# A decayed linear attention with a highway layer behind it: k and q turned in 64-row tiles, q loaded eight tokens to a row, a cap on transfers in flight, and a new order of work

## The chip, the cores and the metric

The kernel runs on one core of a Trainium2 chip. That core has a matrix engine (PE, also TensorE), three engines that work on whole tiles element by element (DVE or VectorE, ACT or ScalarE, POOL or GpSimd), a sequencer that only issues transfers (SP or SyncE), and 16 DMA engines that move data between the chip's main memory and the on-chip memory SBUF. PE reads its operands from SBUF and writes to PSUM, the accumulators, which are divided into banks. Here DVE and ACT read PSUM, and POOL works on SBUF alone.

The metric is the device time of one execution in microseconds (us). Over 13 runs the kernel before takes 109.42 us in the median, 108.25 to 110.27.

## The reference

The inputs are q, k, v of shape 4 batches x 8 heads x 768 tokens x 64, a decay `lam` per head (0.97 to 0.99), two 512 x 512 weights and a bias. Attention is causal and linear, in blocks of 64 tokens with a running state, and the highway layer follows on the 3072 x 512 result.

```python
for b in range(nb):                       # blocks of 64 tokens
    intra = einsum('bhic,bhjc->bhij', qb, kb) * Dmask       # Dmask: lam**(i-j) for i >= j, else 0
    intra = einsum('bhij,bhjd->bhid', intra, vb)
    inter = einsum('bhid,bhde->bhie', qb * lam**(pos+1), kv_state)
    out[:, :, sl] = intra + inter
    kv_state = lam**64 * kv_state + einsum('bhsd,bhse->bhde', kb * lam**(63-pos), vb)
x = out.transpose(0, 2, 1, 3).reshape(3072, 512)
H = maximum(x @ w_h, 0)
T = 1 / (1 + exp(-(x @ w_t + b_t)))
result = T * H + (1 - T) * x
```

## The kernel before

**Stages.** The tokens are cut into 12 stages of 256 tokens, three to a batch, numbered n = 0 to 11. The decay is folded into the operands: q is multiplied by lam to the power of the token's place in its batch and v by lam to the power of minus that place, so the mask has only ones and zeros (`tri`) and the state is a plain running sum, `kv`, which stays in one PSUM bank. A stage has two half-stages b of 128 tokens, and heads are treated in pairs: pair hp is heads 2hp and 2hp+1, and e says which one of the two.

**The order.** Nothing is scheduled by a program. The string `PLAN` is a list of steps, and each engine runs its own steps in the order in which they stand there. A step is `Name.arguments=banks` or `Name.arguments@engine`:

- `Lk`, `Lq`, `Lv`: load half of a stage (256 KB) of k, q or v, all issued by SP in the order of the list; `W`: load half of a weight (512 KB); `ST`: store 256 finished rows (512 KB), also on SP. Five buffers hold raw k, q and v each, so a load can wait for a buffer, and every load behind it on SP then waits as well.
- `CK`, `CQ`, `CV`: cast k to bf16; scale and cast q and v (mostly on POOL). A second argument of 2 means the whole stage. `WC` casts weights.
- `TK`, `TQ`: turn (transpose) k and q on PE by a multiplication with the identity `id128`. One whole-stage step is 8 instructions, each of 128 tokens x 128 features (two heads), which fill all of PE's 128 rows. `EK`, `EQ` copy each PSUM bank of results to SBUF (`kT`, `qT`).
- `SS`: the scores of the head e of all pairs, interleaved with the state update of half-stage 1-e. These are 64 x 64 tiles of PE, so that several can run side by side. `M` multiplies scores by the mask on DVE; `KE` copies the state to SBUF (`ss`).
- `I`: q times state, for each half-stage a group of 4 instructions of 128 columns; `A`: masked scores times v, added to the same bank; `D`: copies the attention output to `xT` in bf16 and puts the tokens back into their order.
- `F.n.u.w`: one block of the highway layer (w=0 for w_h, w=1 for w_t), 8 instructions of 256 columns; `H` (max and subtraction, DVE), `G` (sigmoid, ACT), `X` (product, DVE) follow.
- `R`: turns `xT` + gated part back to token rows, in 64-row tiles: 32 instructions of 64 columns whose two row halves write to two banks; `E` copies to SBUF. The last half-stage goes through `turn`, `evac_o` and `store` instead.
- `Z.n`: n multiplications of no use, which keep PE busy before data is there; `B`, `BC`: the bias as a column; `PT`: loads ACT's sigmoid table.

**What the loads look like.** k, q and v have one partition per two tokens (`J = 2`), so each row that DMA moves is 2 x 64 x 4 = 512 bytes. On SP a load waits, beside its buffer, for the transfer eight places before it, since eight semaphores are used in turn.

**Layouts that matter below.** `qT` is [128 features of a pair, pair, j, 128], so the 128 columns that a score reads are two runs of 64 elements. In `take` (the step `D`) the output is written with a step of two elements, because j is innermost in the token order.

Of the kernel before, what the change touches and what calls it, by code (L numbers as in the profile page):

```python
# [17 lines left out]
Lk.0.0 Lv.0.1 Lv.0.0 Lq.0.0 Lk.0.1 Lq.0.1 Lv.1.1 CK.0.0@POOL Lq.1.0 Z.12=0 TK.0.0=0 Lq.1.1 CV.0.0@DVE Lk.1.0  # L18
CQ.0.0@POOL EK.0.0@DVE Lv.1.0 CV.0.1@DVE CK.0.1@ACT Lk.1.1 Z.11=1 TQ.0.0=1 B=2 EQ.0.0@ACT CQ.0.1@POOL W.0.1 W.0.0
Z.6=0 TQ.0.1=3 TK.0.1=4 EQ.0.1@DVE U.0.0 EK.0.1@ACT W.1.1 S.0.0=56 KE.0.0@DVE S.0.1=01 CQ.1.2@POOL W.1.0 M.0.0.1 Z.1=3  # L20
U.0.1 I.0=34 M.0.1.1 KE.0.1@ACT Lk.2.1 M.0.0.0 A.0.1 M.0.1.0 TQ.1.2=0 Lq.2.1 CV.1.2@DVE CK.1.2@ACT EQ.1.2@ACT Lq.2.0
Z.8=1 TK.1.2=1 A.0.0 EK.1.2@DVE Lk.2.0 D.0.0@DVE Z.3=5 SS.1.1=56 WC.0.0.1@ACT WC.0.0.0@POOL M.1.1.0 KE.1.0@ACT
WC.0.1.0@POOL D.0.1@ACT Lv.2.1 WC.0.1.1@DVE Z.4=0 SS.1.0=01 M.1.1.1 I.1=35 KE.1.1@ACT Lv.2.0 F.0.0.0=4 WC.1.1.0@DVE PT
M.1.0.1 Lk.3.1 F.0.1.0=6 M.1.0.0 WC.1.0.0@POOL WC.1.0.1@ACT Lk.3.0 WC.1.1.1@DVE A.1.1 A.1.0 BC F.0.0.1=1 H.0.1 Lq.3.1
D.1.1@ACT H.0.0 D.1.0@ACT F.0.1.1=0 Lq.3.0 CQ.2.2@POOL F.1.0.0=2 Lv.3.0 G.0.1@ACT CK.2.2@DVE F.1.0.1=6 Lv.3.1
G.0.0@ACT X.0.1@DVE TQ.2.2=5 Lq.4.0 X.0.0@DVE TK.2.2=4 EQ.2.2@ACT CV.2.2@POOL F.1.1.0=3 Lq.4.1 EK.2.2@DVE G.1.0@ACT
H.1.0 SS.2.0=01 Lk.4.1 H.1.1 CK.3.2@POOL SS.2.1=54 Lk.4.0 M.2.0.1 F.1.1.1=2 KE.2.0@ACT M.2.1.0 Lv.4.0 TK.3.2=3 M.2.1.1
CQ.3.2@POOL G.1.1@ACT I.2=15 M.2.0.0 Lv.4.1 A.2.1 X.1.0@DVE A.2.0 Lk.5.0 R.0=40 D.2.0@ACT D.2.1@DVE CV.3.2@POOL
TQ.3.2=6 E.0.0@ACT Lk.5.1 F.2.1.1=1 E.0.1@ACT EQ.3.2@DVE Lq.5.1 EK.3.2@ACT X.1.1@DVE F.2.1.0=5 CQ.4.2@POOL Lq.5.0
R.1=40 H.2.1 SS.3.1=62 Lv.5.0 F.2.0.0=3 CK.4.2@POOL KE.3.0@ACT M.3.1.1 Lv.5.1 E.1.1@ACT M.3.1.0 SS.3.0=52 E.1.0@ACT  # L30
H.2.0 Lq.6.0 TQ.4.2=0 KE.3.1@ACT CV.4.2@POOL M.3.0.1 TK.4.2=6 G.2.1@ACT Lq.6.1 F.2.0.1=4 M.3.0.0 EQ.4.2@ACT EK.4.2@DVE
Lv.6.0 I.3=32 A.3.0 CK.5.2@POOL A.3.1 Lk.6.1 SS.4.1=56 D.3.0@ACT D.3.1@DVE TK.5.2=0 KE.4.0@ACT M.4.1.1 Lk.6.0
F.3.0.0=2 G.2.0@ACT CQ.5.2@POOL EK.5.2@DVE Lv.6.1 SS.4.0=36 H.3.0 F.3.0.1=0 Lq.8.0 M.4.0.0 CV.5.2@POOL M.4.0.1
TQ.5.2=2 Lk.9.0 G.3.0@ACT F.3.1.0=3 X.2.1@DVE Lq.7.0 EQ.5.2@ACT X.2.0@DVE F.3.1.1=6 CQ.6.2@POOL M.4.1.0 Lq.7.1
KE.4.1@ACT I.4=14 H.3.1 G.3.1@ACT R.2=25 Lk.8.1 X.3.0@DVE A.4.0 E.2.1@ACT X.3.1@DVE A.4.1 Lk.7.1 SS.5.0=30 E.2.0@ACT
D.4.0@DVE CK.6.2@POOL SS.5.1=56 D.4.1@ACT Lk.7.0 TQ.6.2=2 M.5.0.0 KE.5.0@ACT CV.6.2@POOL TK.6.2=1 M.5.1.1 Lv.7.0
EQ.6.2@ACT F.4.1.0=4 M.5.0.1 Lv.7.1 EK.6.2@ACT F.4.0.0=3 H.4.1 Lk.8.0 M.5.1.0 I.5=62 SS.6.1=01 H.4.0 Lq.8.1 A.5.0
KE.6.0@ACT M.6.1.0 CQ.7.2@POOL R.3=45 Lv.9.1 A.5.1 M.6.1.1 SS.6.0=30 D.5.0@ACT Lv.8.0 F.4.0.1=1 M.6.0.0 D.5.1@ACT
M.6.0.1 Lk.9.1 TQ.7.2=6 G.4.0@ACT CK.7.2@POOL F.5.0.0=3 Lq.10.1 EQ.7.2@ACT F.4.1.1=2 H.5.0 Lk.10.1 E.3.1@ACT X.4.0@DVE
TK.7.2=0 CV.7.2@POOL G.4.1@ACT I.6=63 ST.0 KE.6.1@DVE F.5.0.1=5 X.4.1@DVE Lv.8.1 F.5.1.0=1 G.5.0@ACT CK.8.2@POOL  # L40
EK.7.2@DVE Lq.9.0 A.6.0 E.3.0@ACT H.5.1 A.6.1 SS.7.1=20 Lq.9.1 D.6.0@ACT D.6.1@DVE TK.8.2=4 M.7.1.1 F.6.1.0=1 Lv.9.0
# [24 lines left out]
def kernel(  # L66
# [13 lines left out]
    C = 128  # L80
# [4 lines left out]
    J = 2  # L85
    N = B * NST
# [12 lines left out]
    def copy(eng, dst, src):  # L99
        if eng == "ACT":  # L100
            A.activation(dst, src, AF.Copy)  # L101
        else:
            ENG[eng].tensor_copy(dst, src)  # L103


    lam_bc = singles.tile([128, H], F32)
    A.dma_start(out=lam_bc, in_=lam.partition_broadcast(128))
    bt_r = singles.tile([KC, 128], F32)
    A.dma_start(out=bt_r, in_=moe_b_t.rearrange("(j p) -> j p", p=128))
    id128 = singles.tile([128, 128], BF16)  # L110
    make_identity(nc, id128)
    blank = singles.tile([128, 512], BF16)
# [306 lines left out]
```

## Time and profile before

| | us or share |
|---|---|
| median of 13 runs | 109.42 |
| the profiled execution, its own time | 109.43 |
| its span, first to last instruction | 107.4 |
| PE busy | 100.0 (93%) |
| DVE busy | 82.3 (77%) |
| ACT busy | 71.8 (67%) |
| POOL busy | 55.7 (52%) |
| moved by DMA | 27.59 MB, of which 20.98 MB read |
| packets under 2 KB | 38712 of 42701 |
| granted PE clock, mean | 0.994 |

The busy time of PE includes the `Z` steps (13.0 us) and modelled ends of matmuls, so it is not the share at which PE does useful work. What a step costs in a row of others is better read from the chain of waits, which gives the time from one step's start to the next one's. DMA busy is the mean over the 16 engines; the shares of the stretches can exceed one since packets on an engine overlap. About 2.0 us of the profiled execution lie outside its span.

### The profile page before, as it was taken

What the parts mean: (1) busy time and instruction counts of PE and PEld (TensorE: products, weight loads), DVE (VectorE), ACT (ScalarE), POOL (GpSimd) and SP (SyncE); (2) the same over time, 40 slices, a digit from 0 to 9 for tenths busy, and PEclk for the clock granted to TensorE, in tenths of its full rate; (3) what the DMA queues carried; (4) which work ended last, traced back from release to release, by engine and by line L of the source; (5) the groups of instructions that cost most, each with busy time, mean ns of one, the idle gap of its engine ahead of it and who ended that gap; (6) DMA issues with size and microseconds to landing.
All of it is one profiled execution on the core that took longest, in us unless ns stands there. A gap on an engine that the chain in (4) does not pass through costs nothing.

```text
span 107.4 us, 4968 instructions
## 1 busy us (share of the span) xinstructions
PE 100.0 (93%) x2188; PEld 80.9 (75%) x2190; DVE 82.3 (77%) x140; ACT 71.8 (67%) x129; POOL 55.7 (52%) x46
## 2 busy tenths in 40 slices
PE   4999989899999999999999799999999999999950
PEld 1344655488987888889888688999898888889930
DVE  1053495879799787999995786999977998958860
ACT  2213244686875688499679495987697798687940
POOL 7028340427989976986658647999791330000000
PEclk9999999999999999999999999999999999999997
DMA  1699999999999999999999799999989354108264
GB/s 35 187 308 291 292 355 387 325 287 275 281 289 270 306 290 281 279 283 264 292 298 284 219 327 316 311 333 307 368 300 290 146 198 165 40 6 321 76 241 150
DMA packets 42701, 27.59 MB, mean 257 GB/s; under 512 B 1588, under 2 KB 38712, under 8 KB 42680
## 3 DMA queue, kind: packets, MB, share of 16 engines
q1 hardware_dynamic: 42528, 27.27, 86.1%
q8 instruction: 17, 0.28, 1.1%
q14 instruction: 4, 0.03, 0.1%
q10 hardware_dynamic: 152, 0.01, 0.1%
HBM read 20.98 MB, written 6.29 MB: 254 GB/s over the span
## 4 chain that ended last, share of the span: by engine, by line
PE 77%; DVE 7%; DMA 5%; issue 3%; POOL 1%; SPq 1%; ACT 1%; DVEq 0%; POOLq 0%
PE bt L300 18%; PE bh L300 18%; PE bs L216 8%; PE bo L281 6%; PE bx L347 6%; PE bqtr L204 6%; DMA qf<-in_q_dram 5%; PE bspin L366 4%; PE bktr L204 4%; PE bo L271 4%; DVE m L255 4%; PE kv L221 2%; DVE hm L305 1%; POOL qb L190 1%; DVE th L318 1%
## 5 line engine op out<-in xcount | busy, mean ns | idle before, releaser
L300 PEld LDWEIGHTS <-w_b 128*128 128x128 bf16 x416 | 36.4, 98 | 4.5
L255 DVE TENSOR_TENSOR m<-bs,tri 128x512 bf16<-128x512 f32 x48 | 31.0, 680 | 2.2 <-PE bs L216 1.9
L190 POOL TENSOR_TENSOR qb<-qf,pow_q 128x1024 bf16<-128x1024 f32 (+1 forms) x13 | 23.5, 1811 | 9.1 <-DMA qf<-in_q_dram 8.2
L314 ACT ACTIVATE bt<-bt,bt_col 128x256 f32<-128x256 f32 (+1 forms) x52 | 22.0, 433 | 6.5 <-PE bt L300 3.9
L300 PE MATMUL bh<-xT,w_b 128*128 128x256 bf16 (+1 forms) x208 | 25.0, 265 | 0.0
L300 PE MATMUL bt<-xT,w_b 128*128 128x256 bf16 (+1 forms) x208 | 24.5, 265 | 0.0
L190 POOL TENSOR_TENSOR vs<-vf,pow_v 128x1024 bf16<-128x1024 f32 x10 | 19.0, 1902 | 6.5 <-DMA vf<-in_v_dram 5.3
L305 DVE SCALAR_TENSOR_TENSOR hm<-bh,xT 128x512 bf16<-128x512 f32 (+1 forms) x26 | 16.5, 643 | 4.6 <-PE bh L300 3.2
L318 DVE TENSOR_TENSOR th<-bt,hm 128x512 bf16<-128x512 f32 (+1 forms) x26 | 16.4, 642 | 2.1 <-ACT bt L314 2.0
L366 PE MATMUL bspin<-blank,id 128*128 128x512 bf16 x43 | 13.0, 451 | 1.6 <-POOL id masks.py:199 1.4
L103 POOL CAST kb<-kf 128x1024 bf16<-128x1024 f32 (+1 forms) x10 | 9.9, 994 | 8.6 <-DMA kf<-in_k_dram 7.7
L101 ACT ACTIVATE xT<-bo 128x512 bf16<-128x512 f32 x16 | 11.6, 748 | 4.2 <-PE bo L281 4.2
L216 PE MATMUL bs<-qT,kT 64*64 64x128 bf16 x384 | 13.8, 218 | 0.3
L101 ACT ACTIVATE ss<-kv 128x512 bf16<-128x512 f32 x15 | 8.9, 596 | 6.0 <-PE bs L216 4.8
L216 PEld LDWEIGHTS <-kT 64*64 64x64 bf16 x384 | 10.9, 106 | 2.6 <-issue 1.1
L101 ACT ACTIVATE o<-bx 128x512 f32<-128x512 f32 x19 | 10.4, 595 | 1.4 <-PE bx L347 1.3
L101 ACT ACTIVATE qT<-bqtr 128x1024 bf16<-128x1024 bf16 (+1 forms) x10 | 9.8, 981 | 1.8 <-PE bqtr L204 1.8
L366 PEld LDWEIGHTS <-id 128*128 128x128 bf16 x45 | 4.6, 111 | 7.1 <-issue 2.8
L281 PE MATMUL bo<-m,vs 64*64 64x128 bf16 x384 | 9.1, 219 | 0.4 <-DVE m L255 0.4
L221 PE MATMUL kv<-vs,kb 64*64 64x64 bf16 x320 | 9.1, 196 | 0.0
L101 ACT ACTIVATE kT<-bktr 128x1024 bf16<-128x1024 bf16 (+1 forms) x7 | 6.8, 973 | 2.0 <-PE bktr L204 2.0
L281 PEld LDWEIGHTS <-vs 64*64 64x64 bf16 x384 | 6.5, 106 | 2.1 <-issue 1.2
(50 smaller groups left out, 110.0 us busy)
## 6 DMA issues: line engine op xcount, KB each, us to landing
kf<-in_k_dram SPq DMA_DIRECT2D x24, 256.0 KB, 5.4
vf<-in_v_dram SPq DMA_DIRECT2D x24, 256.0 KB, 5.3
qf<-in_q_dram SPq DMA_DIRECT2D x24, 256.0 KB, 5.5
out_dram<-o SPq DMA_DIRECT2D x11, 512.0 KB, 4.4
w_f<-in_moe_w_h_dram SPq DMA_DIRECT2D x2, 512.0 KB, 6.7
w_f<-in_moe_w_t_dram SPq DMA_DIRECT2D x2, 512.0 KB, 8.7
out_dram<-oh SPq DMA_DIRECT2D x2, 128.0 KB, 2.0
out_dram<-oq SPq DMA_DIRECT2D x1, 256.0 KB
```

What stands on the lines that cost most here:

```text
L101: A.activation(dst, src, AF.Copy)
L190: ENG[eng].tensor_tensor(dst, in0=get(src, n)[:, heads(p)].rearrange("p h (j d) -> p h j d", j=J), in1=pw[:, n % NST, heads(p), :, None].t ...
L204: T.transpose(t[:, i, j, :], get(x + "b", n)[:, j, h:h + 2, :], id128)
L216: T.matmul(get("s", n, e, hp // 2)[half(b), hp % 2, j, :], lhsT=get("kT", n)[half(e), hp, j, half(b)], rhs=get("qT", n)[half(e), hp, :, ha ...
L221: T.matmul(kv[half(e), hp, half(e)], lhsT=get("kb", n)[half(b), j, 2 * hp + e, :], rhs=get("vs", n)[half(b), 2 * hp + e, j, :], start=firs ...
L255: V.tensor_tensor(new(("m", n, e, u), [128, 2, J, C]), in0=get("s", n, e, u), in1=tri[:, None].to_broadcast([128, 2, J, C]), op=ALU.mult)
L281: T.matmul(get("o", n, b)[half(e), hp, :], lhsT=get("vs", n)[half(b), 2 * hp + e, j, :], rhs=get("m", n, e, u)[half(b), hp % 2, j, :], sta ...
L300: T.matmul(t[:, r, :], lhsT=w_b[w][:, kc, (2 * u + r) * 128:(2 * u + r + 1) * 128], rhs=get("xT", *g)[:, kc, :], start=(kc == 0), stop=(kc ...
L305: V.scalar_tensor_tensor(new(("hm", g, u), [128, 2, z * C], tag=f"hm{z}"), in0=get("h", g, u), scalar=0.0, in1=get("xT", *g)[:, 2 * u:2 * ...
L314: A.activation(dst[:, r, :], src[:, r, :], AF.Sigmoid, bias=bt_col[:, 2 * u + r:2 * u + r + 1])
L318: ENG[eng].tensor_tensor(new(("th", g), [128, NP, z * C], tag=f"th{z}")[:, 2 * u:2 * u + 2, :], in0=get("tt", g, u), in1=get("hm", g, u), ...
L366: T.matmul(t, lhsT=id128, rhs=blank, start=True, stop=True)
```

## The change

Four things change together.

1. **k and q are turned in 64-row tiles.** One step `T` takes the place of `TK` and `TQ`: for k 16 and for q 16 instructions, each of 64 rows, alternating between the two row halves b of PE. Half b writes to its own bank, k in the first 512 elements and q in the second, and `ET.n.2.b` copies a bank ([128, 1024] in bf16, as before) to the tile `T`, which holds [k, q] per half-stage.
2. **q is loaded eight tokens to a row** (`Q = 8`): partitions are (group of eight tokens, head pair), and each row is 8 x 64 x 4 = 2048 bytes. A half load `Lq.n.p` is now head p of every pair. `pow_q` is made anew for this layout, with a second small load of `lam` and a few small set-up instructions. The columns of a turned q are (eight, sixteen groups, pair): scores and `I` read 128 columns with a step of four elements (8 bytes). The mask is built in the new token order, and `D` writes with a step of eight elements (16 bytes) instead of two.
3. **A cap**: from the fifteenth transfer on, each transfer issued by SP also waits until the fifth last has landed.
4. **A new PLAN.** The number of blocks, score steps, masks, stores and `Z` instructions (47) is the same. Nine loads of k and q now stand ahead of the first v, `B`, `BC` and `PT` come early, first turns and scores are re-ordered, and from `F.0.0.0` on the sequence of all steps is new.

```diff
-Lk.0.0 Lv.0.1 Lv.0.0 Lq.0.0 Lk.0.1 Lq.0.1 Lv.1.1 CK.0.0@POOL Lq.1.0 Z.12=0 TK.0.0=0 Lq.1.1 CV.0.0@DVE Lk.1.0
-CQ.0.0@POOL EK.0.0@DVE Lv.1.0 CV.0.1@DVE CK.0.1@ACT Lk.1.1 Z.11=1 TQ.0.0=1 B=2 EQ.0.0@ACT CQ.0.1@POOL W.0.1 W.0.0
...
-R.1=40 H.2.1 SS.3.1=62 Lv.5.0 F.2.0.0=3 CK.4.2@POOL KE.3.0@ACT M.3.1.1 Lv.5.1 E.1.1@ACT M.3.1.0 SS.3.0=52 E.1.0@ACT
-H.2.0 Lq.6.0 TQ.4.2=0 KE.3.1@ACT CV.4.2@POOL M.3.0.1 TK.4.2=6 G.2.1@ACT Lq.6.1 F.2.0.1=4 M.3.0.0 EQ.4.2@ACT EK.4.2@DVE
...
+Lk.0.1 Lq.0.0 Lq.2.1 Lq.1.1 Lq.1.0 Lq.0.1 Lk.0.0 Lk.1.1 Lk.1.0 Z.8=0 B=0 CK.0.1@ACT BC PT TK.0.1=12 Lv.0.0
+Lv.0.1 CQ.1.2@POOL CQ.0.0@DVE Lv.1.0 CK.0.0@DVE Lv.1.1 Z.13=0 TQ.0.0=34 CQ.0.1@POOL TK.0.0 Lk.2.0 ET.0.0.1@DVE
+Z.2=0 TQ.0.1 ET.0.1.1@ACT ET.0.1.0@DVE W.0.1 ET.0.0.0@ACT CK.1.2@ACT Z.6=0 S.0.1=56 W.0.0 S.0.0=04 M.0.0.1 CV.0.1@POOL
+Lq.2.0 CV.0.0@DVE Lk.2.1 M.0.1.0 Z.7=1 U.0.0 T.1.2=12 CV.1.2@POOL M.0.0.0 Lv.2.1 KE.0.0@ACT M.0.1.1 ET.1.2.1@ACT Z.1=3
+I.0=35 A.0.0 ET.1.2.0@DVE Lv.2.0 U.0.1 A.0.1 WC.0.1.1@ACT D.0.1@DVE KE.0.1@ACT W.1.1 D.0.0@ACT Z.6=0 SS.1.1=40
+WC.0.0.1@POOL Lq.3.1 KE.1.0@ACT M.1.1.1 WC.0.1.0@POOL WC.0.0.0@DVE Z.4=1 SS.1.0=62 CQ.2.2@POOL Lq.3.0 I.1=15 M.1.0.0
+F.0.0.0=3 CK.2.2@ACT W.1.0 M.1.1.0 M.1.0.1 Lk.3.0 KE.1.1@ACT T.2.2=06 A.1.1 CV.2.2@POOL Lv.3.0 ET.2.2.1@ACT
...
+CQ.5.2@POOL T.4.2=14 KE.3.1@ACT Lq.6.1 F.3.1.0=3 ET.4.2.0@DVE E.1.1@ACT G.2.1@ACT ET.4.2.1@DVE F.3.0.0=2 Lq.7.1 H.3.1
+SS.4.1=51 CK.5.2@POOL H.3.0 Lv.6.0 F.3.0.1=4 KE.4.0@ACT M.4.1.1 Lk.6.0 E.1.0@ACT X.2.1@DVE SS.4.0=32 G.3.0@ACT Lv.6.1
...
+    Q = 8
...
+    A.dma_start(out=lam_bc[:, H:H + 2], in_=lam.rearrange("(h x) -> h x", x=2)[None].to_broadcast([32, NP, 2]))
...
+    def dma(dst, src, eng=None):
+        i = (eng or nc.sync).dma_start(out=dst, in_=src)
+        if len(issued) >= 14:
+            tc.add_manual_dep(i.ins, issued[-5].ins.name, ...
+        issued.append(i)
...
+        if x == "q":
+            dst = new(("qf", n), [128, 2, Q * D], F32)
+            dma(dst[:, p], q[b, :, ts, :].rearrange("(h x) (o j) d -> x o h (j d)", x=2, j=Q)[p])
...
-                T.transpose(t[:, i, j, :], get(x + "b", n)[:, j, h:h + 2, :], id128)
...
+                    for b in range(2):
+                        T.transpose(t[b][:, i, j, :], get("kb", n)[half(b), j, h:h + 2, :], id128[half(b), half(b)])
...
+            for i in range(Q if p == 2 else Q // 2):
+                for b in range(2):
+                    T.transpose(t[b][:, i, :], get("qb", n)[half(b), i + (4 if p == 1 else 0)], id128[half(b), half(b)])
...
+    def kT(n, b, hp):
+        return get("T", n)[:, b, 0].rearrange("p (h j i) -> p h j i", h=NP, j=J)[:, hp]
+
+    def qT(n, b, hp):
+        return get("T", n)[:, b, 1].rearrange("p (i h) -> p i h", h=NP)[:, :, hp]
...
-        copy(eng, new(("xT", *g), [128, NP, z * C], tag=f"xT{z}")[:, :, r * C:(r + 1) * C].rearrange("p n (q j) -> p n j q", j=J),
-             get("o", n, b).rearrange("p n (j q) -> p n j q", j=J))
+        copy(eng, new(("xT", *g), [128, NP, z * C], tag=f"xT{z}")[:, :, r * C:(r + 1) * C].rearrange("p n (q j) -> p n j q", j=Q),
+             get("o", n, b).rearrange("p n (j q) -> p n j q", j=Q))
```

## The prediction

> **What bounds the kernel now.** I read the engines' totals first, then the busy time by stretches, then the chain of waits step by step, and last the groups by shape and the waits.
>
> ```profile
> PE 100.0 (93%) x2188; PEld 80.9 (75%) x2190; DVE 82.3 (77%) x140; ACT 71.8 (67%) x129; POOL 55.7 (52%) x46
> ```
> ```profile
> 25.00:60.00 35.00, 34.02 (x820) 29.70 (x818) 30.84 (x49) 26.65 (x48) 27.32 (x17) 1.00 1.01 280
> 60.00:80.00 20.00, 20.00 (x500) 17.79 (x499) 17.59 (x30) 14.81 (x26) 16.17 (x11) 1.00 1.05 318
> 95.00:100.00 5.00, 5.00 (x91) 4.68 (x84) 4.02 (x7) 4.13 (x11) 0.00 (x0) 1.00 0.58 213
> ```
>
> The columns are stretch, length, then busy us of PE, weight loads, DVE, ACT, POOL, then clock, DMA share and GB/s. From 25 to 100 us PE has hardly a gap, DVE is right behind it (about 88%), and DMA is full (share 1.0) at 280 GB/s until the loads end. So PE's sequence sets the pace, with DVE and DMA close enough to take over. The chain shows what one step costs inside that sequence:
>
> ```profile
> 44.62 0.98 PE bt L300 x8
> 45.60 0.45 PE bqtr L204 x8
> 46.05 0.87 PE bh L300 x8
> 46.92 0.87 PE bt L300 x8
> 47.79 0.45 PE bo L271 x8
> 48.24 0.57 PE bx L347 x32
> 48.81 0.57 PE bo L281 x32
> ...
> 50.14 0.55 PE bqtr L204 x8
> 50.69 0.45 PE bktr L204 x8
> ```
>
> Second column: us until the next piece. A block of 8 takes 0.87 us after work of the same tile shape and 0.98 after scores; a turn of 8 takes 0.45 after a full-array step and 0.55 after scores. So a change of tile shape costs PE about 0.11 us. L347 is the output's turn, 32 instructions in 64-row tiles: 0.57 with its shape change, so 0.46 by itself.
>
> **The first part: 64-row turns.** Per stage this removes TK and TQ, 0.45 + 0.45 = 0.90 us on the path, and adds 32 instructions of 64 rows and 64 columns in two alternating row halves and two banks. That is the form, count and size of L347, so I take its 0.46. Saved: 0.44 per stage. Counting from `F.0.0.0` (at 22.3 us; both plans have done the same steps by then) ten stages remain: 4.4 us. All other PE steps from there on are equal in number and size. Bounds: if the two halves do not run beside each other, 32 x 64 columns are as many as 16 x 128 and nothing is saved; if the fixed part vanished, not more than 0.5 per stage.
>
> Against it stand shape changes. Counted down both plans from `F.0.0.0`, successive PE steps change shape 47 times before and 59 after, since a turn no longer matches the blocks round it: 12 x 0.11 = 1.3 us more. [...] Net of this part: -3.1 us. PE by itself then needs 76.4 us from `F.0.0.0` to its last turn, where the same sum for before gives 79.5 and the trace shows 81.7 (22.3 to 104.0): 2.2 us of stalls.
>
> **Evacuations.** ET copies the same 1024 elements as EK and EQ did (1.02 us on ACT, 0.69 on DVE), twice a stage: no cost. By steps in the plan from `F.0.0.0` on, DVE loses 4 KE and one CK and gains 3 D, 2 E and 2 ET; ACT gains 5 KE and 2 WC and loses 3 D and 2 E and 2 turned copies. At the rows' durations less the overlap of neighbours (four L255 take 2.48, 0.62 each), DVE has 72.9 us both times and ACT 67. These were hidden under PE's 81.7; under some 78.6 they are still hidden, but DVE's cover falls from 8.8 to 5.7 us.
>
> **D writes with a step of 16 bytes.** Not in the trace. The rows:
>
> ```profile
> L101 ACT ACTIVATE xT<-bo 128x512 bf16<-128x512 f32 x16 | 11.6, 748 | 4.2 <-PE bo L281 4.2
> L101 ACT ACTIVATE ss<-kv 128x512 bf16<-128x512 f32 x15 | 8.9, 596 | 6.0 <-PE bs L216 4.8
> L103 DVE CAST xT<-bo 128x512 bf16<-128x512 f32 x8 | 5.8, 729 | 0.6 <-PE bo L281 0.6
> L103 DVE CAST ss<-kv 128x512 bf16<-128x512 f32 x5 | 3.4, 682 | 0.2 <-PE kv L221 0.2
> ```
>
> A 4-byte step costs ACT 152 ns over a write without step, and DVE 47 ns. From below: the price of no step (a gain of 0.15 and 0.05); from above: double the instruction, +0.75 and +0.73. I take +0.1 each, nearest to the 4-byte row. Ten D on DVE and twelve on ACT: 1 us on each engine, beside PE, of which I put 0.6 on the path, because a block waits for D and DVE's cover has shrunk. [...]
>
> **Scores and I read q with a step of 8 bytes.** No matmul in the trace has such an operand; all their moving columns are contiguous. Bounds: nothing, or half rate. 20 SS at about 0.43 and ten I at 0.45 or 0.22 make 12 us, so half rate costs 12. The nearest rows, the DVE copies with and without a step, differ by 7%. At PE I take zero, since it reads one element per column either way, and keep +12 as a rival.
>
> **q in rows of 2 KB.** The loads of 512-byte rows fill DMA at 280 GB/s; the stores of 2 KB rows reach 213 GB/s at a share of 0.58, so 367 at a full share. At that rate a q half takes 0.71 us instead of 0.94, for 24 halves 5.4 us of DMA time. It is worth nothing on PE's path unless loads are late; it pays for the faster pace. CQ has 1024 elements in runs of 64 as before: 1.90 on POOL.
>
> **Five in flight.** SP's queue holds loads and stores in one order; a wait holds up everything behind it, and behind that POOL, which waited 21.2 us for loads in all (8.2 for qf, 7.7 for kf, 5.3 for vf), 8.8 us of it before 26 us (the rest found PE with other work). A load lands 5.4 us after issue while 280 GB/s means one per 0.94: some 5.8 are in flight. If DMA is full, five keep it full and land sooner (4.7 us): no cost. If latency stays at 5.4, the rate falls to 5 x 0.262 MB / 5.4 us = 243 GB/s. I take the first, because the share of 1.0 says that the engines, not the number in flight, set the rate.
>
> **The start.** The first load's wait ends at 5.6, the twelfth's at 15.4: 0.89 us each; the two w_h halves are there 3.8 us later, at 19.1. After the change 14 loads, not 12, precede them: +1.8, less 5 q x 0.2 = 1.0: about 20. Two casts of 0.6 on POOL: 21.2. On the other branch q0 is scaled after the sixth load (10 us), v0 and v1 arrive tenth to thirteenth (13.6 to 16.3), CV on POOL takes 1.9, and two state copies on ACT (0.6 each) stand behind a weight cast that waits for the weights: SS.1.1 and SS.1.0 end at about 21.5. So `F.0.0.0` starts between 21.2 and 23; I take 22.0, a gain of 0.3. The extra `lam` load and set-up instructions of some 0.2 us end before POOL and DVE have data; 0, or 0.5 if ACT's table load slips behind them.
>
> **The end.** Last block to end of span took 7.0 us (100.4 to 107.4), in before partly a backlog of ACT and DVE; the same steps remain. 0, or 0.5 either way.
>
> **Sum.** -4.4 + 1.3 + 0.6 - 0.3 = -2.8 on a profiled execution of 109.43 us (span 107.4 and 2.0 outside; it stands at the median, 109.42): 106.6.
>
> **Rivals.**
> 1. *DVE becomes the bound.* If D costs twice, DVE rises by 7.3 us to 80.2 from `F.0.0.0`, over PE's 76.4; with the same 2 us of stalls the gain is gone: 108.4 to 110. For: DVE is at 88%. Against: the 4-byte step cost it 7%.
> 2. *Slower: late loads under the cap.* By 82 us 21.0 MB of input and four stores (2.1 MB) must have passed. At 280 and 367 GB/s that is 12.6/0.28 + 10.5/0.367 = 74 us from 2.5 on: 76, so 6 us to spare. At 5/5.8 of the rate it is 86 us, ends at 88, 6 us late: 112.5. It decides from a loss of about 8%, and cancels the gain at 12%. Against: the share of 1.0.
> 3. *Stepped reads slow PE.* Up to 118.6; it cancels the gain from 25% more per score. Against: no evidence either way in the trace.
> 4. *The turns do not run in pairs.* Then 1.3 + 0.6 - 0.3 is left: 111. Against: L347 starts two instructions every 29 ns.
>
> **How the numbers follow.** Forecast 0.60 (own range 104.8 to 108.3: start and tail ±1, stalls ±1), DVE 0.14, cap 0.10, stepped reads 0.10, no pairs 0.06. A measurement of this kernel can tell about 0.5% (0.55 us) from no change. Faster: 0.60 + 0.06 of the DVE case = 0.66; same 0.06; slower 0.28. The range 104.8 to 111.6 leaves out half of the cap case, nearly all of stepped reads and a little below.
>
> **What would show it.** Right: a turn of 32 at about 0.57 on the chain, SS and I unchanged, first block near 22 us, last load before 82 us. Wrong: xT copies over 1 us and DVE without gaps; POOL waiting for kf or vf after 40 us; SS near 1 us; a turn near 1 us. A new order can also have a stall that no row of before shows.

## The result, and the profile after

The changed kernel takes 141.81 us in the median of 11 runs (140.08 to 143.63); the kernel before took 109.22 in 48 runs beside it (108.19 to 110.79). The ratio is 1.294, with a 95% interval of 1.289 to 1.299. The prediction was 106.6 with a range up to 111.6. Times here are medians over all executions of a kernel, while ratios and their intervals compare only the executions in the faster of two states of the chip, so a ratio is not always that of the two medians. The profiled execution has a span of 140.4 us, against 107.4.

First the engines' totals of the page, then the groups by shape (busy us in all, mean ns of one, then the idle time before them):

```profile
PE 116.3 (83%) x2381; PEld 90.3 (64%) x2384; DVE 103.4 (74%) x145; ACT 92.2 (66%) x130; POOL 56.6 (40%) x47
```
```profile
L101 ACT ACTIVATE xT<-bo 128x512 bf16<-128x512 f32 x13 | 31.6, 2512 | 3.6 <-PE bo L323 3.5
L103 DVE CAST xT<-bo 128x512 bf16<-128x512 f32 x11 | 26.8, 2440 | 3.8 <-PE bo L323 3.8
L258 PE MATMUL bs<-kT 64*64 64x128 bf16 x384 | 23.6, 289 | 1.1 <-ACT xT L101 1.0
L313 PE MATMUL bo<-kT,ss 128*128 128x128 bf16 x80 | 11.2, 292 | 0.2 <-ACT ss L101 0.2
```

`D`, the copy of a half-stage's output to `xT`, takes 2.51 us on ACT and 2.44 on DVE, where it took 0.75 and 0.73. The matmuls that read q (scores, L258, and `I`, L313) rose from a mean of 218 and 219 ns to 289 and 292; these are their rows in the kernel before:

```profile
L216 PE MATMUL bs<-qT,kT 64*64 64x128 bf16 x384 | 13.8, 218 | 0.3
L271 PE MATMUL bo<-qT,ss 128*128 128x128 bf16 x80 | 6.4, 219 | 0.8 <-DVE ss L103 0.8
```

PE is busy for longer and yet for a smaller share of the span: it waits. The chain of waits shows for what (start, us until the next piece):

```profile
47.40 0.46 PE bo L313 x4
47.86 0.63 PE bo L323 x32
48.49 0.02 issue
48.51 2.47 ACT xT L101
50.98 0.04 issue
51.02 1.91 PE bh L342 x16
...
55.96 0.34 PE btr L239 x16
56.30 0.23 PE btr L244 x16
56.54 1.02 PE bo L313 x8
57.55 0.88 PE bt L342 x8
58.43 0.63 PE bo L323 x32
59.06 0.02 issue
59.08 2.48 ACT xT L101
```

Masked scores times v (L323) end, PE then stands for 2.47 us until `D` has written `xT`, and the block that reads it (L342) follows. All `D` on the chain are 19% of the span, some 27 us. Between them two things can be read: the turns take 0.34 + 0.23 = 0.57 us a stage, as forecast; an `I` group of 8 takes 1.02 us in place of 0.45, which was not.

Beside that the loads stop for 22 us, as the stretches (stretch, length, busy us of PE, weight loads, DVE, ACT, POOL, clock, DMA share, GB/s) and the wait of SP's queue show:

```profile
25.00:60.00 35.00, 31.65 (x717) 26.30 (x712) 30.31 (x41) 24.11 (x35) 22.64 (x15) 1.00 1.00 300
60.00:85.00 25.00, 20.36 (x516) 16.80 (x512) 19.77 (x29) 19.16 (x25) 10.93 (x7) 1.00 0.24 80
```
```profile
SPq L190 <- DVE o L103: 45.0, 4, 22.1
```

A store, issued by SP in the order of the plan, waits 22.1 us for its rows, and all loads behind it wait as well. This follows from the late blocks and does not cause them: run 1 below takes the slow `D` away and PE then has no gap from 60 to 110 us, although DMA is at a share of 0.51 and 0.45.

### The profile page after: what moved, and what is told of

The parts are those of the page before. It is cut to its first block, busy times and chain, and to the rows that moved or that the text cites. A ratio compares the mean times of both kernels' runs of the same rounds, so it can differ in the third digit from the quotient of the medians.

```text
span 140.4 us, 5368 instructions
## 1 busy us (share of the span) xinstructions
PE 116.3 (83%) x2381; PEld 90.3 (64%) x2384; DVE 103.4 (74%) x145; ACT 92.2 (66%) x130; POOL 56.6 (40%) x47
## 4 chain that ended last, share of the span: by engine, by line
PE 59%; DVE 15%; ACT 13%; issue 6%; DMA 4%; ACTq 0%; DVEq 0%
PE bh L342 13%; PE bt L342 12%; ACT xT L101 10%; DVE xT L103 9%; PE bs L258 9%; PE bspin L408 8%; PE bo L313 6%; PE bo L323 4%; DMA lam_bc<-in_lam_dram 4%; PE bx L389 3%; DVE m L297 2%; PE btr L239 2%; DVE th L360 2%; DVE hm L347 2%; PE kv L263 1%
## 5 line engine op out<-in xcount | busy, mean ns | idle before, releaser
L342 PEld LDWEIGHTS <-w_b 128*128 128x128 bf16 x416 | 38.1, 102 | 17.9 <-DVE xT L103 6.9
L101 ACT ACTIVATE xT<-bo 128x512 bf16<-128x512 f32 x13 | 31.6, 2512 | 3.6 <-PE bo L323 3.5
L342 PE MATMUL bh<-xT,w_b 128*128 128x256 bf16 (+1 forms) x208 | 25.4, 272 | 8.2 <-ACT xT L101 7.3
L103 DVE CAST xT<-bo 128x512 bf16<-128x512 f32 x11 | 26.8, 2440 | 3.8 <-PE bo L323 3.8
L342 PE MATMUL bt<-xT,w_b 128*128 128x256 bf16 (+1 forms) x208 | 25.8, 273 | 2.8 <-DVE xT L103 1.8
L226 POOL TENSOR_TENSOR vs<-vf,pow_v 128x1024 bf16<-128x1024 f32 (+1 forms) x12 | 22.0, 1831 | 12.6 <-issue 5.9
L258 PE MATMUL bs<-kT 64*64 64x128 bf16 x384 | 23.6, 289 | 1.1 <-ACT xT L101 1.0
L101 ACT ACTIVATE ss<-kv 128x512 bf16<-128x512 f32 x20 | 13.4, 670 | 11.9 <-PE bs L258 9.4
L258 PEld LDWEIGHTS <-kT 64*64 64x64 bf16 x384 | 18.4, 120 | 3.5 <-issue 2.5
L101 ACT ACTIVATE kT<-btr 128x1024 bf16<-128x1024 bf16 (+1 forms) x15 | 14.2, 967 | 9.5 <-PE btr L244 9.5
L263 PEld LDWEIGHTS <-kb 64*64 64x64 bf16 x320 | 10.8, 107 | 1.6 <-issue 1.6
L313 PE MATMUL bo<-kT,ss 128*128 128x128 bf16 x80 | 11.2, 292 | 0.2 <-ACT ss L101 0.2
L103 POOL CAST kb<-kf 128x1024 bf16<-128x1024 f32 x9 | 9.3, 1036 | 2.4 <-DVE hm L347 2.4
(55 smaller groups left out, 106.6 us busy)
```

The source lines that it names most:

```text
L226: ENG[eng].tensor_tensor(new(("vs", n), [128, H, J, D])[:, heads(p)], in0=get("vf", n)[:, heads(p)].rearrange("p h (j d) -> p h j d", j=J) ...
L258: T.matmul(get("s", n, e, hp // 2)[half(b), hp % 2, j, :], lhsT=kT(n, b, hp)[half(e), j, :], rhs=qT(n, b, hp)[half(e)], start=True, stop=True)
L263: T.matmul(kv[half(e), hp, half(e)], lhsT=get("kb", n)[half(b), j, 2 * hp + e, :], rhs=get("vs", n)[half(b), 2 * hp + e, j, :], start=firs ...
L313: T.matmul(get("o", n, b)[:, hp, :], lhsT=get("ss", n, b)[:, hp, :], rhs=qT(n, b, hp), start=hp == 0, stop=False, skip_group_check=True)
L342: T.matmul(t[:, r, :], lhsT=w_b[w][:, kc, (2 * u + r) * 128:(2 * u + r + 1) * 128], rhs=get("xT", *g)[:, kc, :], start=(kc == 0), stop=(kc ...
```

## The experiments

### 1 to 3: each stepped access by itself

In run 1 `D` writes with the old step of 4 bytes; in run 2 scores and `I` read unbroken columns of q; run 3 does both. Nothing else in the changed kernel differs. Which token a column stands for does, so these three do not compute the reference's result; the sizes and numbers of all instructions stay.

```diff
# 1 and 3
-        ... .rearrange("p n (q j) -> p n j q", j=Q), get("o", n, b).rearrange("p n (j q) -> p n j q", j=Q))
+        ... .rearrange("p n (q j) -> p n j q", j=J), get("o", n, b).rearrange("p n (j q) -> p n j q", j=J))
# 2 and 3, in qT
-        return get("T", n)[:, b, 1].rearrange("p (i h) -> p i h", h=NP)[:, :, hp]
+        return get("T", n)[:, b, 1].rearrange("p (h i) -> p h i", h=NP)[:, hp]
```

> The changed kernel, with D alone written as before (a step of 4 bytes instead of 16; the token order of the output is then left wrong inside each half-stage, nothing else is left out). Theory A, the write step of D is the main cause: each of the 24 D falls from 2.44-2.51 us to about 0.75, the 26 us of xT copies on the chain go, and the time is 113 to 118 us. Theory B, the stepped reads of PE are the main cause: D was only in the way of engines that had time, and the time stays above 130. Theory C, the order with its loads behind stores is the cause: the pause of 22 us in the loads stays, and the time is above 130.

> The changed kernel, with scores and I reading 128 columns side by side instead of every fourth one (the columns are then those of other tokens and pairs, so the output is wrong; sizes and number are the same), D unchanged. Theory B: SS falls from 1.03 to 0.57 and I from 0.93 to 0.45, 24 x 0.46 + 10 x 0.48 = 16 us, and the time is about 126. Theory A: PE is waiting for D anyway, the steps get as much shorter, but the time stays at 134 to 141.

> Both edits together (output wrong in both ways); what is left of the change is the 64-row turns, the rows of 2 KB, the cap and the order. Theory A+B: these are as good as was forecast, 105 to 108 us, with no pause in the loads, since the pause came from stores that waited for late D and blocks. Theory C: order and cap cost something by themselves, and the time is above 112.

| | us (median) | ratio to before, interval | D on ACT, DVE (ns) | mean score matmul (ns) |
|---|---|---|---|---|
| changed kernel | 141.81 | 1.294 (1.289 to 1.299) | 2512, 2440 | 289 |
| 1: D at 4 bytes | 121.89 | 1.113 (1.100 to 1.127) | 747, 735 | 289 |
| 2: q unbroken | 135.01 | 1.233 (1.216 to 1.250) | 2506, 2434 | 226 |
| 3: both | 110.99 | 1.010 (0.999 to 1.021) | 747, 730 | 218 |

Going from the changed kernel over run 1 to run 3, the step of `D` is worth 19.9 us and the step of the score reads 10.9; in the other order 6.8 for the reads and 24.0 for `D`. The two overlap, since while `D` holds PE up a slower score costs less. Together they are 30.8 of the 32.6 us lost; the other 1.8 are not clear of zero (0.999 to 1.021).

Part of this may be the clock. In the stretches of the profiles the granted clock of PE is 0.50 to 0.51 for 6.8 us of the changed kernel (101.9 to 105.3 and 129.3 to 132.7) and for 13.6 us of run 2, while the rows of run 3 show no such stretch before its end; the means over the profiled executions are 0.973, 0.936 and 0.995. By an estimate from these lengths, if PE set the pace there, up to half of them (3.4 and 6.8 us) would be the clock's and not the step's own. Whether the waits of PE bring the lower clock on, no run tests.

### 4: the price of a step

The kernel before as a bench: `D` of stage n writes with a step of 1, 2, 4, 8 or 16 elements, one half-stage on ACT and one on DVE, and some stages make one run over the whole row in place of many short ones; scores and `I` read q with a step of 1, 2, 4 or 8 elements by stage. Other columns are read and written than the computation wants. In the diff `long` is 1 where one long run is written.

```diff
+    def step_q(n, hp, b):
+        s = (1, 2, 4, 8)[n % 4]
+        v = get("qT", n).rearrange("p n j i -> p (n j i)").rearrange("p (i s) -> p s i", s=s)
+        at = 2 * hp + b
+        return v[:, at % s, at // s * 128:at // s * 128 + 128]
...
+        s, long = ((1, 0), (2, 0), (4, 0), (8, 0), (16, 0), (8, 1), (4, 1), (16, 1), (2, 1), (1, 0), (8, 0), (2, 0))[n]
```

> The kernel before as a measuring bench (output wrong): D of stages 0 to 8 writes with steps of 1, 2, 4, 8, 16 elements in short runs and 8, 4, 16, 2 in runs as long as they can be, always one D on ACT and one on DVE; scores and I of stage n read q with a step of 1, 2, 4, 8 elements for n mod 4 = 0 to 3. If the step in bytes sets the price: D about 0.6, 0.75, then rising to 2.4 us at 16 bytes, the same for long and short runs; SS 0.57 at 1, and 1.03 at 4. If short runs are the price (16 elements at step 8), long runs at 16 bytes are near 0.75. Open: whether a step of 2 or 4 elements is still free for PE (0.57) and for D, and whether PE's price goes on rising at 8.

The timeline of ACT, one `D` each with steps of 2, 4, 8, 16 and 32 bytes, and then 16 bytes in one long run:

```profile
18.50 0.60 ACT L101 ACTIVATE xT<-bo 128x512 bf16<-128x512 f32 x1 [1.23 <-PE bo L287]
24.62 0.75 ACT L101 ACTIVATE xT<-bo 128x512 bf16<-128x512 f32 x1 [0.31 <-PE bo L287]
34.50 1.32 ACT L101 ACTIVATE xT<-bo 128x512 bf16<-128x512 f32 x1 [1.01 <-PE bo L287]
46.62 2.45 ACT L101 ACTIVATE xT<-bo 128x512 bf16<-128x512 f32 x1 [0.94 <-PE bo L287]
55.97 2.35 ACT L101 ACTIVATE xT<-bo 128x512 bf16<-128x512 f32 x1
63.40 2.47 ACT L101 ACTIVATE xT<-bo 128x512 bf16<-128x512 f32 x1 [0.50 <-PE bo L287]
```

And of PE, `I` with a step of 16 bytes (4 instructions) and with none (8 instructions):

```profile
44.94 1.07 PE L277 MATMUL bo<-qT,ss 128*128 128x128 bf16 x4
53.78 0.61 PE L277 MATMUL bo<-qT,ss 128*128 128x128 bf16 x8
```

| step of bf16 in SBUF | D on ACT, us | D on DVE, us | a pair of scores on PE, us |
|---|---|---|---|
| 2 bytes (none) | 0.60 | 0.68 | 0.055 |
| 4 bytes | 0.75 | 0.72 | 0.055 |
| 8 bytes | 1.32 | 1.30 | 0.11 (changed kernel) |
| 16 bytes | 2.45 | 2.44 | 0.225 |
| 32 bytes | 2.35 | 2.33 | not tried |

The last column is the distance from one pair's start to the next in a row of scores; a pair is two 64 x 64 instructions that run side by side (in the timeline of PE two start at 46.47 and 46.48 and last 0.22 us each). From 4 bytes on the price about doubles with the step, for writes and for PE's reads; for the writes it stops at 16 bytes. Long runs cost as much as short ones with the same step (at 16 bytes 2.47 us in place of 2.45 on ACT and 2.47 in place of 2.44 on DVE), so it is the step and not the length of a run. Everything written and read here is bf16, so whether the price goes by bytes or by elements is not shown.

### 5 to 8: the other parts, one at a time

Run 5 puts only the paired turns into the old plan: each `TK` and `TQ` pair becomes one `T`, at the place of the second of them, with two `ET`.

```diff
-TQ.3.2=6 E.0.0@ACT Lk.5.1 F.2.1.1=1 E.0.1@ACT EQ.3.2@DVE Lq.5.1 EK.3.2@ACT X.1.1@DVE
+T.3.2=63 E.0.0@ACT Lk.5.1 F.2.1.1=1 E.0.1@ACT ET.3.2.0@DVE Lq.5.1 ET.3.2.1@ACT X.1.1@DVE
```

> The kernel before with the 64-row turns alone: its plan, its loads, its layouts; where its later turn of a stage stood there is one T with two banks, and ET in the places of EK and EQ (for stage 7 T stands three PE steps later, because no second bank is free). A correct kernel. If the term for the turns was right (0.44 us saved per stage from F.0.0.0 on, 62 changes of tile shape against 47, at 0.11): -4.4 + 1.7 = -2.7, so 106 to 107.5 us. If the turns do not pay in a whole kernel (q must wait for k or the other way round, two banks are held at once, DVE is too near): 109 to 111.

It took 119.58 us, ratio 1.085 (1.078 to 1.093). The turns are short, but the old plan turned k and q at two places, with other steps between them. Now a bank holds both and each copy needs both, and the copies stand on the chain (profile of an execution of 122.76 us), of which they are 8.6 us on ACT, against 0.6 before:

```profile
75.97 1.01 ACT kT L100
83.21 1.03 ACT kT L100
90.07 1.01 ACT kT L100
98.55 1.94 ACT kT L100 x2
```

So in this place of the old order the shorter turns lose more than they save. One arrangement was tried; whether another place in the old order would keep their gain is not shown.

Run 6 puts only the cap into the kernel before (the same rule, `issued[-5]`, for every transfer on SP).

> The kernel before with the cap alone (from the fifteenth transfer on each waits for the fifth last). My term was 0: same within 0.5%, loads landing about 4.7 us after issue instead of 5.4. The rival of late loads: 111 to 113, with POOL waiting longer for kf and vf after 40 us.

110.7 us, ratio 1.0055 (1.0001 to 1.0109). Loads of k, v and q land (from issue until the data is there) after 4.7, 5.0 and 5.1 us, in place of 5.4, 5.3 and 5.5. They land sooner, as forecast, and by the interval the cap costs between nothing and 1.1%.

Run 7 has the new plan, turns and cap, but q in the old layout of two tokens to a row, so scores read unbroken columns and `D` writes with 4 bytes; run 8 is the same without the cap.

```diff
# 7 against the changed kernel, in load
-        if x == "q":
-            dst = new(("qf", n), [128, 2, Q * D], F32)
-            ...
# 8 besides
-        if len(issued) >= 14:
-            tc.add_manual_dep(...)
```

> The changed kernel with q loaded two tokens to a row as before, hence with contiguous reads of q and D at a step of 4 bytes: 64-row turns, cap and new order remain. A correct kernel. Against the run with both edits (111.0) the only difference is that q comes in rows of 512 bytes: if rows of 2 KB are worth 0.2 us per half load at the start, where ten loads stand ahead of the weights, 112 to 113; if the order of the casts there sets it, 110 to 111. That it beats the kernel before would need a start as early as before (first block at 22.3), which I do not expect.

> The same without the cap. If the cap is free: within 0.5% of the run with it. If the cap made the weights late at the start (they are the fifteenth and sixteenth transfer, the first that it holds): the first block about 1 us earlier and the time 1 us shorter. If the cap helps by keeping the queue short: longer.

112.23 us, ratio 1.025 (1.017 to 1.032), and 111.89, ratio 1.024 (1.018 to 1.029). The cap makes no difference here either. The chain of run 7 goes from transfer to transfer between 10 and 57 us; that of run 3, with the long rows, does not. That does not show that loads set the time of run 7: with the cap each transfer waits for an earlier one, and in run 6 transfers are 66% of the chain at a time level with before. In run 8, without the cap and at the same time as run 7, PE is 75% of the chain and transfers 5%. Against run 3 the rows of 2 KB are worth some 1.2 us (112.23 against 110.99), hardly clear of the noise (1.017 to 1.032 against 0.999 to 1.021), and that comparison also changes the set-up of `pow_q` and the mask.

### 9 to 11: the same values, with the step on the other side

Run 9 computes what the changed kernel computes, but reorders while reading PSUM: `D` writes in unbroken order and reads its bank with a step of 64 bytes; `ET` is cut into k's half and q's half, and q's half is written unbroken. Run 10 has besides another order at the start. Run 11 is the kernel before with `D` reordering on the side that it reads.

```diff
# 9, in take
-        ... xT ... .rearrange("p n (q j) -> p n j q", j=Q), get("o", n, b).rearrange("p n (j q) -> p n j q", j=Q))
+        ... xT ... .rearrange("p n (q j) -> p n q j", j=Q), get("o", n, b).rearrange("p n (j q) -> p n q j", j=Q))
# 9, in evac_t
+        copy(eng, dst[:, 0, es], t[:, 0])
+        copy(eng, dst[:, 1].rearrange("p (h i) -> p h i", h=NP)[:, :, js], t[:, 1].rearrange("p (i h) -> p h i", h=NP))
# 10 besides: Z.13 to Z.9, Z.6 and Z.7 to Z.4, CV.0.0@DVE ahead of ET.0.0.1@DVE,
#   WC.0.0.0@DVE right behind D.0.1@DVE, W.1.0 behind W.1.1, WC.1.0.0 on ACT
# 11, in take, with j=J
-        ... xT ... .rearrange("p n (q j) -> p n j q", j=J), get("o", n, b).rearrange("p n (j q) -> p n j q", j=J))
+        ... xT ... .rearrange("p n (q j) -> p n q j", j=J), get("o", n, b).rearrange("p n (j q) -> p n q j", j=J))
```

> The changed kernel, but the copies that reorder do so on the side they read: D writes xT in unbroken order and reads its PSUM bank with a step of 16 float32 (64 bytes); the copy of a turned stage is split into k's half and q's half, and q's half reads its bank with a step of 8 bytes and writes q unbroken, so that the score and I matmuls read unbroken columns. The same values are computed. Theory A (the price lies on a stepped write into SBUF and on TensorE's stepped read of SBUF, and a stepped read of PSUM by ScalarE or VectorE costs little): D 0.6 to 0.75 us, the four-pair score group 0.22 to 0.25 us of reads, about 24 more copies, on ACT and DVE, of 0.4 to 0.7 us beside TensorE; time 109 to 112.5 us, that of the run with both steps taken away or a little more. Theory B (any stepped access costs by its bytes, reads of PSUM too): D stays over 1.2 us, q's half over 0.9 us, and the time is 118 to 140 us.

> As the run before it, with the start put in another order: fewer spins (Z.13 to Z.9, Z.6 to Z.4, Z.7 to Z.4), the scaling of v in chunk 0 ahead of the second copy of the turned chunk on VectorE, the cast of the first block's second weights right behind the first D, W.1.0 loaded right behind W.1.1, and one cast from VectorE to ScalarE. If what is left of the difference (111.0 against 109.2 with both steps gone) is the late first blocks (F.0.0.0 at 24.9 us instead of 22.3, behind a cast of its weights on VectorE): F.0.0.0 at 22.5 to 23.5 us and the time 1 to 2.5 us under that of the run before it, 107 to 110 us. If the rest lies in the steady part, or the lost spins leave TensorE at a lower clock: within 0.7 us of the run before it, or slower.

> The kernel before, with one edit: D writes xT in unbroken order and reads its PSUM bank with a step (every second float32 of the token order there, 8 bytes or more apart) instead of writing with a step of 4 bytes. Same values. Theory A (stepped reads of PSUM cost little): D 0.60 on ScalarE and 0.68 to 0.72 on VectorE instead of 0.75 and 0.73; since TensorE bounds that kernel, 108.6 to 109.4 us (ratio 0.994 to 1.001). Theory B: D over 1 us and 112 to 122 us.

The groups of run 9:

```profile
L101 ACT ACTIVATE xT<-bo 128x512 bf16<-128x512 f32 x13 | 7.5, 597 | 1.9 <-PE bo L326 1.9
L103 DVE CAST xT<-bo 128x512 bf16<-128x512 f32 x11 | 7.5, 683 | 0.4 <-PE bo L326 0.4
```

A read of float32 from PSUM with a step of 64 bytes costs ACT and DVE nothing: 597 and 683 ns are the price of a copy without any step. The banks of turned k and q hold bf16, and there it is not free on DVE. In run 10 the two halves of one `ET` are, k's without a step and q's with one of 8 bytes:

```profile
54.02 0.42 DVE L103 COPY kT<-btr 128x512 bf16<-128x512 bf16 x1
54.36 0.68 DVE L103 COPY kT<-btr 128x512 bf16<-128x512 bf16 x1
```

On ACT both halves take 0.59 to 0.60. A step of 8 bytes in float32 is free on DVE (685 ns in run 11, against 682 for a copy without one). With the cut, one `ET` on DVE takes 1.01 us in place of 0.68, so from run 9 on the edit itself adds work on DVE: its copies of turned k and q are 10.1 us in run 10 and 6.9 in run 3. Run 9 took 111.45 us (1.019, 1.014 to 1.025), run 10 109.85 (1.001, 0.996 to 1.005), run 11 109.25 (1.001, 0.998 to 1.004). So theory A held for `D` and for the scores, but not for q's half on DVE, and 30 us of the loss go away by moving the step to the other operand. Run 11 shows that `D` was not on the path in the kernel before: 0.15 us off each ACT `D` moved nothing.

Run 9 is still 1.6 us over run 10, and its chain says why:

```profile
23.00 1.79 DVE w_b L103
24.79 0.05 issue
24.83 0.54 PE bh L345 x4
```

The first block (at 24.83, where it was 22.3 before) waits for the cast of its weights, which takes DVE 1.79 us while POOL scales v (22.59 to 24.49); the same cast takes 0.42 in run 10. Run 10 casts earlier and has its first block at 23.35.

### 12 to 15: where the turns' gain goes

Run 10 is level with the kernel before although the turns are in it. PE's busy time without the `Z` steps is 100.0 - 13.0 = 87.0 us before and 96.2 - 12.5 = 83.7 in run 10: 3.3 us less, and the span is not. (`Z` has to be taken out, since its number is not the same: the plan before has 45 such instructions and that of the changed kernel 47.) Not all of it lies where the forecast put it. From the first block to the end of the span PE is busy for 80.4 of 85.25 us before and for 78.6 of 84.61 in run 10, 1.8 less; the stretch is 0.6 shorter, and it begins 1.0 later. Run 12 loads stage 0's q, k and v first; run 13 moves two turned copies from DVE to ACT besides; runs 14 and 15 are these two without the cap.

```diff
# 12
-Lk.0.1 Lq.0.0 Lq.2.1 Lq.1.1 Lq.1.0 Lq.0.1 Lk.0.0 Lk.1.1 Lk.1.0 Z.8=0
+Lk.0.1 Lq.0.0 Lq.0.1 Lk.0.0 Lv.0.0 Lv.0.1 Lq.1.1 Lq.1.0 Lk.1.1 Lk.1.0 Z.8=0
-CQ.1.2@POOL CQ.0.0@DVE ... Z.9=0 TQ.0.0=34 CQ.0.1@POOL
+CQ.0.1@POOL CQ.0.0@DVE ... Z.4=0 TQ.0.0=34 CQ.1.2@POOL
# 13 besides
-ET.4.2.1@DVE  ET.7.2.0@DVE
+ET.4.2.1@ACT  ET.7.2.0@ACT
```

> As the run before it (steps on the read side, start in another order), and the first loads put in the order of their use: both q halves of chunk 0 and its k and v first, those of chunks 1 and 2 behind them, so that the scaling of chunk 0's q on VectorE need not wait for the sixth transfer (it began at 9.84 us and took 1.83); on POOL chunk 0's half of q ahead of chunk 1's; three spins shortened. Theory A (the gain of the turns is lost before the first F block): first scores at 12 to 13.5 us instead of 15.3, F.0.0.0 at 21 to 22.5 instead of 23.4, and the time 1 to 2.5 us lower, 107.3 to 108.9. Theory B (it is lost in the stretches in which VectorE never rests, 43 to 50 and 60 to 70 us): the start is earlier as above, but the time stays within 0.6 us of 109.85.

> As the run before it, with two of the copies of turned stages (ET.4.2.1 and ET.7.2.0, two instructions of 0.55 us each) moved from VectorE to ScalarE in the two stretches where VectorE never rests. Theory A: within 0.5 us of the run before it. Theory B (VectorE holds TensorE there): 0.5 to 1.5 us under the run before it, 106 to 108.5 us.

> The version with the loads in the order of their use (12), without the rule that a transfer is issued only once the fifth last has landed. Theory A (with five in flight the loads of the new order come late: in run 13 loads of k, q and v of 4.2 to 6 us each follow one another on the chain from 37 to 58 us): DMA share back to 1.0 in the steady part, landing 5.0 to 5.5 us, and 0.5 to 2 us lower than 110.09. Theory B (the cap costs nothing here either, as in the order of before and with two tokens per row of q): within 0.5 us of 110.09.

> The version with two copies fewer on VectorE (13), without the rule on transfers in flight. If VectorE and the loads hold TensorE in turn, this one, with both relieved, is the fastest: 107 to 108.8 us. If neither does: 109.5 to 110.7.

| | us (median) | lowest to highest | ratio to before, interval |
|---|---|---|---|
| 12: first stage first | 110.09 | 108.4 to 112.61 | 0.999 (0.994 to 1.004) |
| 13: two copies off DVE | 110.67 | 108.03 to 484.38 | 1.008 (1.002 to 1.014) |
| 14: as 12, no cap | 110.95 | 109.15 to 114.0 | 1.007 (1.001 to 1.013) |
| 15: as 13, no cap | 111.4 | 109.66 to 112.79 | 1.010 (1.002 to 1.018) |

In run 12 the start did what was expected of it: first scores at 13.87 us (15.29 in run 10), first block at 22.4. The time stayed. What was won at the start is lost later. One stretch lies on the chain on DVE alone, shown here from run 12:

```profile
42.61 0.94 DVE kT L103 x3
43.55 1.20 DVE hm L350 x2
44.74 0.60 DVE m L300
45.34 0.60 DVE th L363
45.94 0.46 DVE m L300
46.39 0.06 issue
46.45 1.28 DVE m L300 x2
47.73 0.93 DVE kT L103 x2
```

That speaks for theory B of run 12: from 42.6 to 50.0 us DVE does not rest. Two of the rows are the cut `ET` (L103, `kT`), whose extra work on DVE comes from the edit of run 9 and not from the turns. DVE's busy time from the first block on is 71.1 us before and 74.0 in run 10. No run has the start of run 10 with `ET` uncut, so how much of the gain this extra work ate is not shown.

Run 13 takes work off DVE in that stretch and is not faster, but it decides little. Its executions spread widely (one of 122.58 and one of 484.38 us among 13), so a gain of a few tenths could not be seen in it. In its profile (an execution of 112.64 us) DVE is gone from the chain there and transfers stand one behind the other from 37.5 to 58.0 us; with the cap such a chain does not show that loads set the time, and without it (run 15) PE is 73% of the chain and transfers 12%, at no better a time. None of these versions beats the kernel before. So the turns are shorter and no run shows their gain as time. What keeps it back is seen for the start (run 9) and, by its chain, for DVE in a stretch of run 12; beyond that it stays open, and so does whether an order exists in which it arrives.

## Why the prediction was wrong

The difference to 106.6 is 35.2 us. Over the chain of runs it comes apart as: the step of `D` 19.9, the step of the score reads 10.9, the remainder of run 3 against before 1.8 (not clear of zero), and 2.6 of forecast gain that did not come (109.2 against 106.6). An unknown part of the first, by the estimate above at most 3.4 us, may be the granted clock.

- **"D writes with a step of 16 bytes" failed, in size and in reach.** The step took +0.1 us a copy and called double the instruction the upper end, +0.75 and +0.73. Measured is +1.76 and +1.71, outside the bound. The value was taken by the row that it was nearest to, the 4-byte step, but a price that grows with the step can't be bounded by one row at its cheap end: 4 bytes cost ACT 0.15, 8 bytes 0.72, 16 bytes 1.85. The reach was wrong too: 0.6 us on the path was argued from what DVE has free, but a block waits for the `D` of its own tokens, so PE waits for a longer `D` whatever the engine's share. The 24 `D` grew by 41.7 us in all, and 19.9 to 24.0 us of that, about half, arrived as time. Rival 1, "DVE becomes the bound", had the operation right and the mechanism wrong: DVE went down to 74% busy.
- **"Scores and I read q with a step of 8 bytes": the zero taken for PE failed, and the rival's price was right.** The reason given, one element per column either way, does not hold: 0.11 us a pair in place of 0.055. The 12 us of the rival were 10.9 (6.8 in the other order).
- **The turns: the prices held, the way to time failed.** A stage's turns take 0.57 us with the shape change, against 0.90 before. A change of shape still costs 0.11 in run 10: a block takes 0.98 us after the output's turn (at 80.31) and 0.87 after another block (at 81.29). By these rows the work fell by the 3.1 us of the forecast; PE's busy sum from the first block on fell by 1.8, but its ends are modelled, so it does not decide. Wrong was that PE's sequence alone sets the pace, so that less of it means less time. The margin of DVE and of the loads beside PE was thin, and the views showed this (DVE at 88%, DMA at 1.0); the forecast named it and let the gain through in full. Which of them took the 2.6 us, or whether the extra work of the cut `ET` did, stays open.
- **Evacuations: `ET` costs what `EK` and `EQ` did**, 1.02 us on ACT, as the step had it. The instruction took that in the old order too (run 5, 1.01); there it stood on the chain, and so it was not without cost.
- **Five in flight: right.** Landing fell from 5.4 to 4.9 us in the changed kernel and the cap cost between nothing and 1.1% (run 6), and taking it away gained nothing in runs 8, 14 and 15. Rival 2 did not happen. The idle DMA from 60 to 85 us had another cause, a store waiting on SP ahead of the loads.
- **q in rows of 2 KB: put at nothing on the path, some 1.2 us when tried, hardly clear of the noise.** Whether the order of the new plan needs it is not shown.
- **The start: forecast between 21.2 and 23, and 24.83 with the steps on the side of PSUM (run 9); in the changed kernel 26.6.** In run 9 POOL's two casts of the first weights ended at 20.76, near the 21.2 of the sum, but the block also needs weights that DVE casts, and the sum left that cast out: it stretched to 1.79 us beside POOL. In the changed kernel that cast took 0.66 us and had ended by 25.1, and the block there came behind PE's own steps. The 13 `Z` multiplications ahead of the first turn of q took 5.37 us from 8.25 on, 0.41 each, where the 11 of the kernel before had taken 2.55. The granted clock in the views is 1.00 for both, and why they differ is not shown.

## What to carry to other kernels

When a layout changes which operand is read or written with a step, price the step, on every engine that touches it: for bf16 in SBUF 4 bytes cost little here (ACT 0.60 to 0.75 us, DVE 0.68 to 0.72, a pair of scores 0.055 both ways), 8 about doubled a copy or a matmul (1.32 and 1.30 us, 0.11 a pair), and 16 took about four times as long (2.45 and 2.44 us, 0.225 a pair). If a reordering is needed, try the step on the side of the copy that reads PSUM: from float32 banks a step of 64 bytes cost nothing (0.60 us on ACT, 0.68 on DVE), and from bf16 banks a step of 8 bytes cost nothing on ACT (0.59 to 0.60) but took DVE from 0.42 to 0.68 us. And do not count a saving on the busiest engine in full while the next two have little room; here 3.1 us fewer by the prices of PE's steps did not show as time in any run.

## What the runs showed of the hardware that was not expected

**The price list of steps** above: for bf16 in SBUF it about doubles from 4 to 8 and from 8 to 16 bytes, for ACT's and DVE's writes alike (0.75, 1.32 and 2.45 us on ACT, 0.72, 1.30 and 2.44 on DVE), where it ends for them (2.35 and 2.33 at 32 bytes), and PE pays it on q, the operand of which a score reads 128 columns (0.055, 0.11 and 0.225 us a pair).

**Reads of float32 from PSUM with a step are free for ACT and DVE** (597 and 683 ns at 64 bytes in run 9, 596 and 682 for the state's copy without a step). Of bf16 they are free on ACT (0.59 to 0.60 us), while DVE takes 0.68 us in place of 0.42 (run 10, a step of 8 bytes).

**DVE took longer while POOL worked on SBUF (1.83 us in place of 0.69), and POOL beside DVE (1.55 us, where work of that size took 1.04).** The same instruction, the scale of stage 0's q, in the timelines of DVE and POOL in run 10, then of DVE and POOL in run 12:

```profile
9.84 1.83 DVE L220 TENSOR_TENSOR qb<-qf,pow_q 128x512 bf16<-128x512 f32 x1 [2.03 <-issue]
```
```profile
9.22 3.35 POOL L220 TENSOR_TENSOR qb<-qf,pow_q 128x1024 bf16<-128x1024 f32 x2 [6.16 <-DMA qf<-in_q_dram]
```
```profile
8.78 0.69 DVE L220 TENSOR_TENSOR qb<-qf,pow_q 128x512 bf16<-128x512 f32 x1 [0.50 <-DMA qf<-in_q_dram]
9.41 1.25 DVE L103 CAST kb<-kf 128x512 bf16<-128x512 f32 x1
```
```profile
8.82 1.55 POOL L220 TENSOR_TENSOR qb<-qf,pow_q 128x512 bf16<-128x512 f32 x1 [5.75 <-DMA qf<-in_q_dram]
14.16 1.04 POOL L226 TENSOR_TENSOR vs<-vf,pow_v 128x512 bf16<-128x512 f32 x1
```

In run 10 POOL had begun at 9.22 and DVE's 0.69 became 1.83. In run 12 DVE began 0.04 us ahead, kept its 0.69, and POOL took 1.55 for an amount of work that takes 1.04 elsewhere; DVE's next cast then ended 0.3 us after POOL did. The rows show that the two ran at the same time, not what held either up; no run was made for it alone. DVE's copies from PSUM show nothing of it: the 11 of `xT` take 0.68 to 0.69 us in run 10, six of them with POOL at work beside them.
